# Earlier bias transfers, a staircase moved to VectorE and lent PSUM banks in a fused attention and feed-forward kernel

## The chip, the cores and the metric

The kernel runs on one core of one Trainium2 chip. The metric is the device time of the core in microseconds (us), median of several runs. Ratios are the mean time of one kernel's fast runs over that of the other's of the same rounds, so they are not quite the ratio of the medians that stand beside them. Under 1 is faster. A ratio comes with a 95% interval.

TensorE does the matmuls, VectorE (DVE) and ScalarE (ACT) empty PSUM, GpSimd (POOL) casts inputs and issues small transfers, SyncE (SP) issues the large loads.

## The reference, cut to what matters

```
scores = q k^T / 8                       # 8 x 8 heads, 576 positions, 64 wide, causal
bias   = -(cum[i] - cum[j]),  cum = cumsum(max(s, 0))
attn   = softmax(scores + min(bias, 0))
x      = attn v, heads side by side      # 4608 x 512
h      = x w_in                          # 512 -> 2048
out    = (h * clip(h + 3, 0, 6) / 6) w_out
```

The kernel handles heads in 32 pairs. The feed-forward part, two chains of 512-wide matmuls, is cut into groups that are slipped between the attention steps from pair 4 on. TensorE does all of both.

## The kernel before

The bias enters the scores as four more rows of q and k (rows 64 to 67 of a qk buffer; a constant "staircase" of rows stands behind them, from row 68 on), and a small transfer per head, called aug below, puts them there. There are three qk buffers. The kernel uses eight PSUM banks: two each under the names s, ph and po, one each under t and o. `ph` and `po` belong to the first and the second matmul of the feed-forward part.

```python
def load_aug(p, eng):                       # the bias rows of a pair
    for hh in range(2): eng.dma_start(out=qks[p % NQK][64:68, hh, ...], in_=aug[2*p+hh ...])

def t_bank(other, name):                    # where a transpose lands
    if early[0] and other:                  # early: pairs 0 to 3
        return psum.tile([128, 640], F16, tag="po", bufs=2, name=name)
    return psum.tile([128, 640], F16, tag="t", name=name)

def transpose(p, i):                        # i = 0: q, 1: k;  pairs 0 to 8
    ...                                     # six PE transposes into t_bank(i == 1)
    copy = (nc.vector.tensor_copy, nc.scalar.copy)[i]
    for hh in range(2): copy(out=qk[0:64, hh, i, ...], in_=pt[...])

def av(p, hh, part):                        # attention times v
    if part == 0:
        tag = "t" if hh and p > NPE else "o"
        O[p, hh] = psum.tile([128, 5, 65], F32, tag=tag, bufs=1, name="O")
    ...
for p in range(NP):
    cast_qk(p + 2, gpsimd, gpsimd)          # GpSimd
    if p == 0: set_stair(2, gpsimd)
    else: cast_v(p + 1)
    load_aug(p + 2, nc.gpsimd)
    next_weights(...)                       # GpSimd issues these too
    ...                                     # SyncE: loads of pair p + 3
    if p < PPB:                             # pairs 0 to 3: attention alone
        scores(p,0,0); scores(p,0,1); get(0); scores(p,0,2); corner(p)
        av(p-1,1,0); av(p-1,1,1); norm(p-1,1)
        scores(p,1,0); get(1); scores(p,1,1)
        transpose_x(p-1)
        av(p,0,0); scores(p,1,2); av(p,0,1); norm(p,0)
        continue
    ...                                     # from pair 4 on, with group() between the steps
    corner(p); get(1); group(); scores(p,1,0); group(); ...
```

`get(i)` transposes q or k of the next pair (from pair 9 on it spreads what a DMA transpose brought). `norm` divides by the row sums on VectorE, and `transpose_x` needs its result. `scores(p, hh, 0)` ends with a minimum against a mask on VectorE, `corner` with a smaller one.

The softmax here doesn't subtract the row's maximum and nothing guards it: scores larger than these inputs give would overflow.

Of the kernel before, what the change touches and what calls it, by code (L numbers as in the profile page):

```python
# [9 lines left out]
F32 = mybir.dt.float32  # L10
# [8 lines left out]
def kernel(  # L19
# [10 lines left out]
    nc = tc.nc  # L30
# [7 lines left out]
    NP = NHEADS // 2  # L38
# [92 lines left out]
            in_=v[b, h0 : h0 + 2, 512:SEQ, :].rearrange("h p d -> p h d"),  # L131
        )

    def load_aug(p, eng):
        for hh in range(2):
            g = 2 * p + hh
            eng.dma_start(  # L137
                out=qks[p % NQK][64:68, hh, :, 64 * hh : 64 * hh + SEQ],
                in_=aug[g : g + 1, :, :, :],
            )  # L140
# [39 lines left out]
    def cast_qk(p, eng_q, eng_k):  # L180
        tok = work.tile([128, 24 * D], F16, tag="tok", name="tok")
        if p < NPE:
            tok = tok[0:96].rearrange("p (i e h d) -> p i e h d", i=2, e=6, h=2)
            for i, eng in enumerate((eng_q, eng_k)):
                eng(out=tok[:, i].rearrange("p t h d -> p h t d"), in_=raw6(p)[:, i])  # L185
        else:
            tok = tok[:, 0 : 18 * D]
            for i, eng in enumerate((eng_q, eng_k)):
                eng(  # L189
                    out=tok[:, 9 * D * i : 9 * D * (i + 1)],  # L190
                    in_=raws[p % NRAW][:, 9 * D * i : 9 * D * (i + 1)],
                )
        toks[p] = tok

    def cast_v(p):
        vraw, va = vraws[p % NRAW], vas[p % NQK]
        nc.gpsimd.tensor_copy(out=va[:, :, 0:4, 0:64], in_=vraw[:, :, 0:4, :])  # L197
        nc.gpsimd.tensor_copy(out=va[0:64, :, 4, 0:64], in_=vraw[0:64, :, 4, :])
# [8 lines left out]
        return psum.tile(shape, F32, tag=tag, bufs=2, name=name)  # L207

    def t_bank(other, name):
        if early[0] and other:  # L210
            return psum.tile([128, 640], F16, tag="po", bufs=2, name=name)
        return psum.tile([128, 640], F16, tag="t", name=name)

    def transpose(p, i):
        tok, qk = toks[p], qks[p % NQK]
        pt = t_bank(i == 1, "pt")
        for e in range(6):
            nc.tensor.transpose(  # L218
                pt[:, 96 * e : 96 * (e + 1)],
                tok[:, i, e].rearrange("p h d -> p (h d)"),  # L220
                ident[0:96, 0:96],
            )
        copy = (nc.vector.tensor_copy, nc.scalar.copy)[i]
        for hh in range(2):
            r = 64 * hh
            copy(  # L226
                out=qk[0:64, hh, i, r : r + SEQ].rearrange("p (t e) -> p t e", e=6),
                in_=pt[r : r + 64, 0:SEQ].rearrange("p (e t) -> p t e", e=6),
            )
# [37 lines left out]
    def scores(p, hh, g):  # L267
        qT, kT = qk_of(p, hh)
        pt = Pof(p, hh)
        S = s_bank([128, 512], "S")  # L270
        if g == 0:
            for j in range(4):
                c = slice(128 * j, 128 * (j + 1))
                mm(S[:, c], lhsT=kT[:, c], rhs=qT[:, c], start=(j == 0), stop=(j == 3))  # L274
        else:
            for j in ((0, 3) if g == 1 else (1, 2)):
                c = OFF[j] - 512 * g
                w = 448 - 128 * j
                mm(  # L279
                    S[:, c : c + w],  # L280
                    lhsT=kT[0:68, 128 * j : 128 * (j + 1)],
                    rhs=qT[0:68, 128 * (j + 1) : SEQ],
                    start=(c == 0),
                    stop=(c != 0),
                )
        c = slice(512 * g, 512 * (g + 1))
        nc.scalar.activation(out=pt[:, c], in_=S, func=AF.Exp, scale=0.125)  # L287
        if g == 0:
            nc.vector.tensor_tensor(  # L289
                out=pt[:, c], in0=pt[:, c], in1=masks[:, c], op=ALU.min  # L290
            )
# [22 lines left out]
    def av(p, hh, part):  # L314
        va, pt = vas[p % NQK], Pof(p, hh)
        if part == 0:

            tag = "t" if hh and p > NPE else "o"
            O[p, hh] = psum.tile([128, 5, 65], F32, tag=tag, bufs=1, name="O")
        o = O[p, hh]  # L320

        def block(i, j, lhsT, **kw):
            mm(o[:, i, :], lhsT=lhsT, rhs=va[:, hh, j, 0:65], **kw)  # L323

        def off(i, j):
            c = OFF[j] + 128 * (i - j - 1)
            block(i, j, pt[:, c : c + 128], start=False, stop=False)

        if part == 0:
            for j in range(4):  # L330
                block(j, j, pt[:, 128 * j : 128 * (j + 1)], start=(j == 0), stop=False)
            for i in range(1, 5):
                off(i, 0)
        else:
            for i, j in ((2, 1), (3, 1), (4, 1), (3, 2), (4, 2), (4, 3)):
                off(i, j)
            c = 64 * hh
            block(4, 4, PCs[p % 2][:, c : c + 128], start=False, stop=True)
# [103 lines left out]
    def group():  # L442
        a, c = m1_ready(), m2_ready()
        if not (a or c):
            return False
        if a and (last[0] == 2 or (tail[0] and not c)):
            m1(*m1_list[done[1]])
            done[1] += 1
            last[0] = 1
        else:  # L450
            if c:
                m2(*m2_list[done[2]])
                done[2] += 1
            last[0] = 2
        return True
# [16 lines left out]
    def set_stair(i, copy):  # L472
        for hh in range(2):
            copy(
                out=qks[i][64:128, hh, :, 64 * hh : 64 * hh + 640].rearrange(
                    "p i (t c) -> p i t c", c=128
                ),
                in_=stair_sb[64:128, :, None, :].to_broadcast([64, 2, 5, 128]),
            )
# [36 lines left out]

    cast_qk(0, nc.scalar.copy, nc.scalar.copy)
    transpose(0, 0)
    load_aug(0, nc.scalar)
    transpose(0, 1)  # L520
    cast_v(0)
    cast_qk(1, nc.gpsimd.tensor_copy, nc.gpsimd.tensor_copy)
    next_weights(1)
    load_aug(1, nc.gpsimd)
    cast_v(1)


    for p in range(NP):
        nxt = p + 1 < NP
        if p + 2 < NP:  # L530
            cast_qk(p + 2, nc.gpsimd.tensor_copy, nc.gpsimd.tensor_copy)
            if p + 2 >= NPE:
                crossbar_qk(p + 2)
        if p == 0:
            set_stair(2, nc.gpsimd.tensor_copy)
        elif nxt:
            cast_v(p + 1)
        if p + 2 < NP:
            load_aug(p + 2, nc.gpsimd)
        next_weights(1 if p < 3 else 2 if p < 4 else 3)  # L540
        for m in (p + 3, p + 4):
            if m < NP and (m < NPE) == (m == p + 3):
                for i in range(2):
                    load_qk(m, i, nc.sync)
        if p + 3 < NP:
            load_v(p + 3, nc.sync)

        def get(i):
            if p + 1 < NPE:
                transpose(p + 1, i)  # L550
            elif nxt:
                spread(p + 1, i)

        if p < PPB:
            scores(p, 0, 0)
            scores(p, 0, 1)
            get(0)
            scores(p, 0, 2)
            corner(p)
            if p:  # L560
                av(p - 1, 1, 0)
                av(p - 1, 1, 1)
                norm(p - 1, 1)
            scores(p, 1, 0)
            get(1)
            scores(p, 1, 1)
            if p:
                transpose_x(p - 1)
            av(p, 0, 0)
            scores(p, 1, 2)  # L570
            av(p, 0, 1)
            norm(p, 0)
            continue

        if p == PPB:
            av(p - 1, 1, 0)
            av(p - 1, 1, 1)
            norm(p - 1, 1)
            scores(p, 0, 0)
            scores(p, 0, 1)  # L580
            transpose_x(p - 1)
            early[0] = False
            scores(p, 0, 2)
            get(0)
            group()
            group()
        else:
            scores(p, 0, 0)
            get(0)
            group()  # L590
            scores(p, 0, 1)
            av(p - 1, 1, 0)
            group()
            scores(p, 0, 2)
            av(p - 1, 1, 1)
            norm(p - 1, 1)
            group()
        corner(p)
        get(1)
        group()  # L600
        if p > NPE:
            x_done[0] = p - 1
        scores(p, 1, 0)
        group()
        scores(p, 1, 1)
        av(p, 0, 0)
        if p > PPB:
            (crossbar_x if p >= NPE else transpose_x)(p - 1)
        group()
        scores(p, 1, 2)  # L610
        group()
        av(p, 0, 1)
        norm(p, 0)
        group()
# [40 lines left out]
```

## Time and profile before

| | before |
|---|---|
| time, median of 4 runs | 371.19 us (370.39 to 371.49) |
| span of the profiled run | 367.8 us, TensorE busy 340.9 |
| first scores | 13.59 us |
| first group of the feed-forward part | 38.89 us |
| mean granted TensorE clock | 0.995 |

Two more lines of its page, beside those in the prediction. The first is the chain of work that ended last, as shares of the span by engine. The second is the clock that TensorE was granted, in tenths of full speed per slice of 9.2 us (the digit 8 is one stretch at half speed: 0.75 over the 6.77 us of pair 3 makes about 3.4 us, an estimate).

```profile
PE 80%; DVE 7%; DMA 7%; POOL 2%; ACT 2%; issue 1%; SPq 0%; POOLq 0%; ACTq 0%
PEclk9998999999999999999999999999999999999999
```

### The profile page before, as it was taken

How to read it: one execution, taken by the hardware profiler on the slowest of the kernel's cores; microseconds unless marked ns; L12 is line 12 of the kernel's file. 1: busy time of each engine (PE TensorE's matmuls, PEld its weight loads, DVE VectorE, ACT ScalarE, POOL GpSimd, SP SyncE). 2: the span in 40 equal slices, each digit the busy share in tenths (PEclk: the TensorE clock that was granted, in tenths of full speed). 3: DMA queues.
4: the chain of work that ended last, by engine and by line, in shares of the span. 5: the costliest groups of instructions: out<-in, count | busy, mean ns of one | idle time of the engine just before them, and what ended most of it. 6: DMA issues, size and time to landing. Idle time of an engine off the chain costs nothing.

```text
span 367.8 us, 7622 instructions
## 1 busy us (share of the span) xinstructions
PE 340.9 (93%) x2841; PEld 190.6 (52%) x2841; DVE 242.3 (66%) x544; ACT 225.8 (61%) x392; POOL 120.4 (33%) x217
## 2 busy tenths in 40 slices
PE   1486888999998999999999999999999999999995
PEld 0475555555555555555555555555555444444442
DVE  7477688687778777777777777777775644544531
ACT  6577789766667666666666666666666343343310
POOL 3997694643335342433334333332000000000000
PEclk9998999999999999999999999999999999999999
DMA  8999999999999898998999979987411010010012
GB/s 203 239 229 241 223 229 175 189 192 215 201 176 172 158 192 165 191 177 173 183 153 200 179 165 189 179 176 127 80 48 46 30 57 29 30 59 29 30 57 86
DMA packets 150589, 54.01 MB, mean 147 GB/s; under 512 B 137808, under 2 KB 145632, under 8 KB 150552
## 3 DMA queue, kind: packets, MB, share of 16 engines
q1 hardware_dynamic: 143616, 48.17, 67.5%
q0 software_dynamic: 6272, 4.78, 7.8%
q10 hardware_dynamic: 664, 0.58, 0.6%
q8 instruction: 22, 0.36, 0.4%
q14 instruction: 15, 0.12, 0.1%
HBM read 37.11 MB, written 9.44 MB: 127 GB/s over the span
## 4 chain that ended last, share of the span: by engine, by line
PE 80%; DVE 7%; DMA 7%; POOL 2%; ACT 2%; issue 1%; SPq 0%; POOLq 0%; ACTq 0%
PE po L406 33%; PE ph L386 31%; PE O L323 6%; PE S L279 6%; DMA qk<-aug 3%; DMA vraw<-in_v_dram 3%; PE S L274 3%; DVE gT L395 1%; DVE P L289 1%; DVE qk L226 1%; POOL tok L185 1%; DVE x L346 1%; DVE qk L249 1%; ACT P L287 1%; ACT tr L394 1%
## 5 line engine op out<-in xcount | busy, mean ns | idle before, releaser
L395 DVE SCALAR_TENSOR_TENSOR gT<-tr,ph 128x512 f16<-128x512 f32 x144 | 98.9, 687 | 95.6 <-ACT tr L394 92.2
L386 PE MATMUL ph<-xT,w_in_sb 128*128 128x512 f16 x576 | 147.9, 379 | 0.7 <-DVE gT L395 0.5
L394 ACT ACTIVATE tr<-ph,bias 128x512 f32<-128x512 f32 x144 | 99.0, 688 | 79.7 <-PE ph L386 71.7
L406 PE MATMUL po<-w_out_sb,gT 128*128 128x512 f16 x576 | 145.5, 379 | 0.0
L287 ACT ACTIVATE P<-S 128x512 f16<-128x512 f32 x192 | 112.0, 595 | 39.9 <-PE S L274 22.8
L406 PEld LDWEIGHTS <-gT 128*128 128x128 f16 x576 | 50.3, 97 | 46.1
L386 PEld LDWEIGHTS <-w_in_sb 128*128 128x128 f16 x576 | 51.1, 97 | 44.3 <-issue 0.7
L137 POOL DMA_DIRECT2D qk<-aug x62 | 36.3, 587 | 65.4 <-PE S L279 50.9
L279 PE MATMUL S<-qk 68*128 68x448 f16 (+3 forms) x256 | 51.2, 282 | 0.4 <-ACT P L287 0.2
L323 PE MATMUL O<-va,P 128*128 128x65 f16 x896 | 49.0, 195 | 2.4 <-DVE x L346 2.4
L323 PEld LDWEIGHTS <-P 128*128 128x128 f16 x896 | 40.5, 99 | 16.1 <-DVE x L346 3.6
L197 POOL CAST va<-vraw 128x512 f16<-128x512 f32 x32 | 20.1, 629 | 56.0 <-PE O L323 50.3
L279 PEld LDWEIGHTS <-qk 68*128 68x128 f16 x256 | 24.5, 102 | 24.4 <-issue 1.2
L289 DVE TENSOR_TENSOR P<-P,masks_sb 128x512 f16<-128x512 f16 x64 | 30.4, 476 | 7.3 <-ACT P L287 7.2
L189 POOL CAST tok<-raw 128x576 f16<-128x576 f32 x46 | 29.9, 672 | 12.5 <-DMA raw<-in_q_dram 4.3
L346 DVE TENSOR_TENSOR x<-O,rl 128x320 f16<-128x320 f32 x64 | 31.4, 491 | 2.2
L249 DVE COPY qk<-jt 64x768 f16<-64x768 f16 x92 | 30.7, 334 | 1.7
L274 PE MATMUL S<-qk 128*128 128x128 f16 x256 | 26.0, 227 | 5.9 <-DMA qk<-aug 5.1
L415 DVE TENSOR_SCALAR ob<-po 128x512 f32<-128x512 f32 x36 | 24.6, 682 | 9.5 <-PE po L406 9.5
L274 PEld LDWEIGHTS <-qk 128*128 128x128 f16 x256 | 19.8, 101 | 18.7 <-issue 6.4
L218 PE MATMUL pt<-ident,tok 96*128 96x96 f16 x108 | 9.5, 237 | 10.7 <-ACT tok L185 7.8
L185 POOL CAST tok<-raw 96x768 f16<-96x768 f32 x16 | 13.2, 842 | 6.2 <-PE ptx L360 3.0
(39 smaller groups left out, 141.4 us busy)
## 6 DMA issues: line engine op xcount, KB each, us to landing
raw<-in_q_dram SPq DMA_DIRECT2D x32, 288.0 KB, 3.9
out_dram<-ob SPq DMA_DIRECT2D x36, 256.0 KB, 2.3
raw<-in_k_dram SPq DMA_DIRECT2D x31, 288.0 KB, 7.4
vraw<-in_v_dram SPq DMA_DIRECT2D x64, 128.0 KB, 4.5
w_in_sb<-in_moe_w_in_dram POOLq DMA_DIRECT2D x4, 512.0 KB, 9.8
w_out_sb<-in_moe_w_out_dram POOLq DMA_DIRECT2D x8, 256.0 KB, 8.7
vraw<-in_v_dram SPq DMA_DIRECT2D x32, 32.0 KB, 3.7
qk<-aug POOLq DMA_DIRECT2D x62, 9.0 KB, 3.5
```

The lines of the kernel that those rows point to most:

```text
L137: eng.dma_start(out=qks[p % NQK][64:68, hh, :, 64 * hh : 64 * hh + SEQ], in_=aug[g : g + 1, :, :, :],)
L249: nc.vector.tensor_copy(out=qk[0:64, :, i, 128 * par : 128 * par + 256 * n].rearrange("p h (s two c) -> p h s two c", two=2, c=128)[:, :, ...
L274: mm(S[:, c], lhsT=kT[:, c], rhs=qT[:, c], start=(j == 0), stop=(j == 3))
L279: mm(S[:, c : c + w], lhsT=kT[0:68, 128 * j : 128 * (j + 1)], rhs=qT[0:68, 128 * (j + 1) : SEQ], start=(c == 0), stop=(c != 0),)
L287: nc.scalar.activation(out=pt[:, c], in_=S, func=AF.Exp, scale=0.125)
L289: nc.vector.tensor_tensor(out=pt[:, c], in0=pt[:, c], in1=masks[:, c], op=ALU.min)
L323: mm(o[:, i, :], lhsT=lhsT, rhs=va[:, hh, j, 0:65], **kw)
L346: nc.vector.tensor_tensor(out=X[p][:, :, hh, :], in0=o[:, :, 0:64], in1=rl.to_broadcast([128, 5, 64]), op=ALU.mult,)
L386: mm(ph, lhsT=w_in_sb[:, kc, ft * 128 : (ft + 1) * 128], rhs=xT[:, kc, n * 512 : (n + 1) * 512], start=(kc == 0), stop=(kc == NKC - 1),)
L394: nc.scalar.activation(out=tr, in_=ph, func=AF.Relu, bias=bias3[:, 0:1])
L395: nc.vector.scalar_tensor_tensor(out=gTs[n][:, ft, :], in0=tr, scalar=6.0, in1=ph, op0=ALU.min, op1=ALU.mult)
L406: mm(po, lhsT=gTs[n][:, ft, t4 * 128 : (t4 + 1) * 128], rhs=w_out_sb[:, ft, :], start=(ft == 0), stop=(ft == NFT - 1),)
```

## The change

The intent: bias transfers are issued ahead of the casts in GpSimd's program, pair 0's on two queues. VectorE, idle at that time, makes the third staircase. The idle banks of the second matmul hold the k and x transposes (before, only those of pairs 0 to 3) and the second head's output until the second matmul starts. Half of the k copies of odd pairs goes from ScalarE to VectorE. Cut to its core:

```diff
-        if early[0] and other:
+        if not done[2] and other:
             return psum.tile([128, 640], F16, tag="po", bufs=2, name=name)
...
-        copy = (nc.vector.tensor_copy, nc.scalar.copy)[i]
         for hh in range(2):
+            on_act = i == 1 and (hh == 0 or p % 2 == 0)
+            copy = nc.scalar.copy if on_act else nc.vector.tensor_copy
...
-            tag = "t" if hh and p > NPE else "o"
-            O[p, hh] = psum.tile([128, 5, 65], F32, tag=tag, bufs=1, name="O")
+            tag = "o" if not hh or 0 < done[2] and p <= NPE else "t" if p > NPE else "po"
+            O[p, hh] = psum.tile(
+                [128, 5, 65], F32, tag=tag, bufs=2 if tag == "po" else 1, name="O"
+            )
...
-    load_aug(0, nc.scalar)
+    load_aug(0, (nc.scalar, nc.gpsimd))
     transpose(0, 1)
+    set_stair(2, nc.vector.tensor_copy)
     cast_v(0)
+    load_aug(1, (nc.gpsimd, nc.gpsimd))
     cast_qk(1, nc.gpsimd.tensor_copy, nc.gpsimd.tensor_copy)
...
         if p + 2 < NP:
+            load_aug(p + 2, (nc.gpsimd, nc.gpsimd))
             cast_qk(p + 2, nc.gpsimd.tensor_copy, nc.gpsimd.tensor_copy)
-        if p == 0:
-            set_stair(2, nc.gpsimd.tensor_copy)
-        elif nxt:
+        if p and nxt:
             cast_v(p + 1)
-        if p + 2 < NP:
-            load_aug(p + 2, nc.gpsimd)
...
         corner(p)
-        get(1)
         group()
         scores(p, 1, 0)
+        get(1)
         group()
```

Below, "bias part" means the bias issues and the staircase, "bank part" the banks and the later place of `get(1)`.

More of the change, by code (lines that the diff above doesn't have):

```diff
@@ L132, in load_v, with load_aug @@
         )
-    def load_aug(p, eng):
-        for hh in range(2):
+    def load_aug(p, engs):
+        for hh, eng in enumerate(engs):
             g = 2 * p + hh
@@ L518 @@
     transpose(0, 0)
-    load_aug(0, nc.scalar)
+    load_aug(0, (nc.scalar, nc.gpsimd))
     transpose(0, 1)
+    set_stair(2, nc.vector.tensor_copy)
     cast_v(0)
+    load_aug(1, (nc.gpsimd, nc.gpsimd))
     cast_qk(1, nc.gpsimd.tensor_copy, nc.gpsimd.tensor_copy)
     next_weights(1)
-    load_aug(1, nc.gpsimd)
     cast_v(1)
```

## The prediction

> **What bounds the kernel now.** I read the page first. Its two lines of totals:
>
> ```profile
> PE 340.9 (93%) x2841; PEld 190.6 (52%) x2841; DVE 242.3 (66%) x544; ACT 225.8 (61%) x392; POOL 120.4 (33%) x217
> PE   1486888999998999999999999999999999999995
> ```
>
> TensorE is busy for 340.9 of 367.8 us, and the second line (tenths of busy time in 40 slices) puts its holes into the first third. From there on the end moves only with TensorE's work, which this change leaves as it is (the same 5684 rows in its program, some in another order). So at most the 26.9 us of TensorE's idle time is on offer. The stretches view says where it lies: 12.2 us are before 13.6 us, when the first scores start (7.83 before the first transpose, 4.36 before the scores, little more); some 4 us after the last matmul; 10.7 us between 13.6 and 122 us; from 120 to 280 us there is none. The end needs no look: its last output transfer is not touched.
>
> I then cut the span at the first score matmul of each pair of heads. Columns: stretch, its length, then busy time of TensorE (instructions), its weight loads, VectorE, ScalarE, GpSimd, then granted clock, DMA share, GB/s:
>
> ```profile
> 13.59:18.83 5.24, 4.65 (x46) 3.77 (x46) 3.95 (x5) 4.33 (x9) 5.17 (x8) 1.00 1.19 237
> 18.83:25.19 6.36, 5.58 (x66) 4.62 (x66) 5.13 (x13) 4.93 (x10) 6.32 (x11) 1.00 1.24 225
> 25.19:30.38 5.19, 3.44 (x66) 2.89 (x66) 3.61 (x9) 4.22 (x9) 4.33 (x8) 1.00 1.18 245
> 30.38:37.15 6.77, 5.50 (x80) 4.72 (x81) 5.03 (x12) 5.02 (x10) 5.04 (x8) 0.75 1.20 234
> 37.15:45.04 7.89, 6.59 (x73) 3.99 (x69) 5.16 (x11) 6.33 (x12) 5.78 (x9) 1.00 1.24 231
> 45.04:52.80 7.76, 6.91 (x82) 4.44 (x81) 6.43 (x15) 6.99 (x14) 6.85 (x11) 1.00 1.20 222
> 52.80:60.56 7.76, 6.91 (x82) 4.45 (x81) 6.60 (x15) 6.99 (x14) 3.29 (x6) 1.00 0.97 175
> 60.56:70.27 9.71, 8.62 (x90) 5.22 (x89) 7.64 (x17) 7.32 (x14) 5.20 (x10) 1.00 1.14 206
> ```
>
> Pairs 0 to 3 have attention alone, pairs 4 to 7 have first-matmul groups beside it. TensorE's idle time here (length less busy) is 0.59, 0.78, 1.75, 1.27, 1.30, 0.85, 0.85 and 1.09 us. What ended it, from the timeline, in the brackets:
>
> ```profile
> 13.59 0.59 PE L274 MATMUL S<-qk 128*128 128x128 f16 x4 [4.36 <-DMA qk<-aug]
> 18.73 0.23 PE L323 MATMUL O<-va,PC 128*128 128x65 f16 x1 [0.59 <-DVE PC L308]
> 25.19 0.38 PE L274 MATMUL S<-qk 128*128 128x128 f16 x4 [0.78 <-DMA qk<-aug]
> 29.11 0.45 PE L360 MATMUL ptx<-ident,x 128*128 128x128 f16 x5 [1.61 <-DVE x L346]
> 36.67 0.60 PE L323 MATMUL O<-va,P 128*128 128x65 f16 x14 [0.82 <-DVE x L346]
> 40.76 0.42 PE L218 MATMUL pt<-ident,tok 96*128 96x96 f16 x6 [0.78 <-POOL tok L185]
> 48.52 0.42 PE L218 MATMUL pt<-ident,tok 96*128 96x96 f16 x6 [0.58 <-POOL va L198]
> 56.29 0.41 PE L218 MATMUL pt<-ident,tok 96*128 96x96 f16 x6 [0.58 <-DVE qk L226]
> 64.30 0.42 PE L218 MATMUL pt<-ident,tok 96*128 96x96 f16 x6 [0.83 <-DVE qk L226]
> ```
>
> The last four are one wait: the k transpose wants the single t bank, which VectorE is still emptying of q (its copies end at 40.61, 48.47, 56.23, 64.24). The two rows that name GpSimd are misread releasers; its casts for that pair ended by 32.1 us for the first of them.
>
> **What the Trainium skill says.** (1) "DMA: Bandwidth & Descriptors", section "Issuing engines are not separate DMA queues": starting transfers from several engines saves only issue time. The trace agrees so far: the two bias transfers of pair 0 on ScalarE's queue were issued at 8.31 and about 9.6 us and took about 5.2 us each, as the large loads beside them did (4.7 to 4.9), since the engines are full (share above 1.1). (2) "SBUF — State Buffer", "SBUF: two separate sides": VectorE operations with two SBUF inputs and GpSimd lock each other out. The trace agrees: the mask minimum at 14.84 us took 1.45 us beside a GpSimd cast and 0.41 at 18.60; the corner's minimum at 17.76 took 0.91 beside GpSimd's staircase copy and 0.21 elsewhere. (3) "TensorE: Matmul & The Clock Gate", Part 1: half clock until a window of about 3.4 us was busy. The trace: the 128x64 and 128x448 pair of matmuls took 0.63 us until 22.9 us and 0.38 after, and the 30.38 stretch shows clock 0.75.
>
> **The change, part by part.**
>
> *Bias of pair 0 on two queues.* The first score waits only for head 0, still issued by ScalarE at 8.31 after the bias rows are ready at 8.14. It lands near 13.5 as before. Head 1 leaves GpSimd at about 8.2 instead of ScalarE at 9.6, with some 6 us to landing (GpSimd's took 5.7 to 7.4): 14.3, before its first use at 15.2. The first weight load (512 KB) leaves 1.2 us later, behind two more bias issues of 0.58 us, so a little less traffic is about: 0.1 us.
>
> *Third staircase on VectorE.* 2.53 us leave GpSimd at 16.07 and become about 1.0 us of VectorE at 10.1 (as its first, 2 x 0.5), where VectorE sits idle until 14.84. It frees GpSimd and the lock, so the corner's minimum takes 0.2 instead of 0.9. The 0.59 at 18.73 largely goes. But the odd pair's k half, 0.75 us, comes into VectorE's queue just there: 0.3 us.
>
> *Bias ahead of casts.* Pair 2's bias was issued at 18.54 behind casts and staircase and landed at 25.15; now it goes at about 14.5 and lands by 21. The 0.78 goes, but ScalarE's exponentials of pair 1 last until 25.0, so the chain gains not 0.8 but 0.6. Pair 3's (22.86 to 30.24, on the chain of waits) had landed 0.1 us before TensorE came to it, so no more is gained than not being held later. The 1.61 at 29.11 stays: scores, exponential, mask, 1.51 of q copies, corner, reciprocal, product are a chain through VectorE of 3.9 us.
>
> *Banks lent.* The second head's output no longer waits for the first head's normalisation. At 36.67 half of the 0.82 is covered by the exponentials, which end at 36.5 anyway: 0.5 us. For pairs 4 to 7 the k transposes get a second-matmul bank and come one group later. Their waits sum to 0.78 + 0.58 + 0.58 + 0.83 = 2.77, and three waits of 0.26 to 0.27 for the output bank go too: 3.56.
>
> *k copies shared.* An odd pair moves 0.64 us from ScalarE to 0.75 us on VectorE. ScalarE's 6.99 of 7.76 becomes 6.35 in the 52.80 stretch, but VectorE's 6.60 becomes 7.35. So that pair can fall to about 7.4, not to TensorE's 6.91; the 45.04 one (even, ScalarE 6.99) to about 7.2; 37.15 to 7.1 and 60.56 to 8.95. That is 0.4 + 0.55 + 0.8 + 0.75 = 2.5 us of the 3.56.
>
> *Later groups.* The k spread now follows the next mask and the group's product, so of the 0.53 us wait for the product at 119.35 I take 0.4. Later stretches have no idle time.
>
> Sum: 0.1 + 0.3 + 0.6 + 0.5 + 2.5 + 0.4 = 4.4 us. I take off 0.3 for the k half in VectorE's chain of pairs 1 and 3, and for GpSimd, which now waits for the previous pair's last score before it may cast. 371.2 - 4.1 = 367.1 us.
>
> **Rivals.** (a) *DMA is the early bound.* It moves 220 to 245 GB/s through the first 50 us. Then earlier compute would wait for loads, and about 369.5 would be left. For it: loads issued at 22.7 take 11.8 us. Against it: pair 6's q lands near 38.5 and is transposed at 45.3, so about 5 us of slack exist. (b) *The blocked GpSimd queue turns on us*: casts behind a bias that waits for scores come later, and so do raw buffers and loads: 369 to 372. Against it: the casts of pairs 3 and 5 wait for their loads anyway. (c) *The clock*: with the gaps at 18.73 and 25.19 gone, the half-speed window of 30.4 to 33.8 vanishes or warm-up comes a window sooner; each window holds up to 1.5 us of extra matmul time, most of it now hidden in the VectorE chain. With all of TensorE's waits gone as well: 364.5. The reverse, one more cold window, costs about as much.
>
> **Range and chances.** The floor is about all early waits except the 29.11 one gone (some 6.7 us, 364.5); the ceiling is gains only at the bank (369.6). Faster by over 2% needs under 363.8, which needs every term in full and a clock window: 7%. Slower by 2% has no mechanism of that size: 2%.
>
> **What would show it.** First score still near 13.5; no wait on the bias at pair 2's first score; no wait on q copies at the k transposes of pairs 5 to 8; first product of the second matmul near 62 instead of 65.64; VectorE the busiest helper where an odd pair is copied. It is wrong if the first score moves by over 1 us, if TensorE's waits before 70 us stay above 7 us in sum after 13.6 (8.5 now), or if new idle time turns up after 120 us.

## The result, and the profile after

The changed kernel takes 369.81 us (368.89 to 370.07, 4 runs) against 371.19 us. The ratio is 0.9962, interval 0.9938 to 0.9986. That is 1.4 us where 4.1 were predicted, and just outside the range. In a later call it was 0.9984 (0.993 to 1.0038).

First, the lines of its page that answer to those above: engine totals, TensorE's busy tenths, its clock, and the chain by engine.

```profile
PE 341.5 (93%) x2841; PEld 191.7 (52%) x2841; DVE 250.1 (68%) x550; ACT 222.8 (61%) x388; POOL 117.0 (32%) x216
PE   1478988899998999999999999999999999999995
...
PEclk9995899999999999999999999999999999999999
...
PE 83%; DVE 9%; ACT 4%; DMA 2%; issue 1%; ACTq 0%
```

Transfers fall from 7% to 2% of the chain, as intended. But VectorE's and ScalarE's shares rise together by about as much as TensorE's, and the clock row holds a 5 and an 8 where there was one 8: from the clocks below some 10.2 us at half speed instead of 3.4 (an estimate). The record misses the start, where the clock reads 1.00 while matmuls take the half-speed time. By the matmuls' own durations TensorE was slow for about 17 us (14.35 to 21.4 and 28.8 to 38.5) instead of about 13 (13.6 to 23.5 and 30.4 to 33.9). TensorE is busy for longer (341.5) although its work is the same.

The stretches from pair to pair, same columns as in the prediction:

```profile
14.35:18.76 4.41, 4.41 (x45) 3.72 (x46) 3.12 (x6) 3.50 (x8) 4.41 (x8) 1.00 1.16 223
18.76:24.19 5.43, 4.61 (x69) 3.93 (x67) 4.66 (x11) 4.48 (x9) 4.86 (x8) 1.00 1.18 237
24.19:30.55 6.36, 4.08 (x72) 3.54 (x69) 5.50 (x11) 3.85 (x10) 4.32 (x7) 0.83 1.20 230
30.55:37.95 7.40, 6.91 (x84) 5.88 (x82) 6.19 (x12) 5.29 (x10) 4.63 (x8) 0.50 1.24 235
37.95:44.63 6.68, 6.63 (x71) 4.17 (x69) 5.96 (x13) 5.45 (x11) 5.34 (x9) 0.95 1.23 231
44.63:52.62 7.99, 6.79 (x82) 4.45 (x81) 7.18 (x15) 7.21 (x14) 6.43 (x11) 1.00 1.21 211
52.62:59.85 7.23, 6.80 (x82) 4.45 (x81) 7.05 (x16) 6.34 (x13) 4.66 (x9) 1.00 1.16 202
59.85:69.74 9.89, 8.53 (x91) 5.21 (x90) 7.80 (x17) 7.17 (x14) 4.28 (x8) 1.00 0.99 200
```

Pairs 0 and 1 are 0.83 and 0.93 us shorter than before (5.24 and 6.36). Pairs 2 and 3 are 1.17 and 0.63 us longer (5.19 and 6.77), and pair 3 runs wholly at clock 0.50. Pairs 4 to 7 take 31.79 us together instead of 33.12. TensorE's waits, from its timeline:

```profile
14.35 0.58 PE L275 MATMUL S<-qk 128*128 128x128 f16 x4 [5.11 <-DMA qk<-aug]
23.21 0.45 PE L363 MATMUL ptx<-ident,x 128*128 128x128 f16 x5 [0.82 <-DVE x L349]
28.77 0.72 PE L363 MATMUL ptx<-ident,x 128*128 128x128 f16 x5 [2.28 <-DVE x L349]
35.25 0.72 PE L363 MATMUL ptx<-ident,x 128*128 128x128 f16 x5 [0.49 <-DVE x L349]
50.17 0.45 PE L363 MATMUL ptx<-ident,x 128*128 128x128 f16 x5 [1.20 <-DVE x L349]
57.40 0.45 PE L363 MATMUL ptx<-ident,x 128*128 128x128 f16 x5 [0.43 <-DVE x L349]
65.09 1.04 PE L409 MATMUL po<-w_out_sb,gT 128*128 128x512 f16 x4 [1.36 <-DVE x L349]
...
118.73 0.34 PE L275 MATMUL S<-qk 128*128 128x128 f16 x3 [0.92 <-DVE qk L250]
```

Every wait that the change aimed at is gone: the bias at pair 2, the corner minimum, the four on the t bank, the output bank. In their place stand waits for one thing, x on VectorE: the normalisation, met at the x transpose, and at 65.09 by the first second-matmul, whose bank still holds the last lent output. From 76 to 109 us the changed kernel is 0.86 us ahead (pair 12's second-head scores start at 108.76 instead of 109.61). At 118.73 it waits for the k spread, and by 123.7 us the lead is 0.03. So the changed kernel's run stands against the other as follows: start 0.76 us lost, pairs 0 to 3 0.04 lost, pairs 4 to 7 1.33 won, pair 8 0.33 won, pairs 9 to 14 0.83 lost. They end at the same span, 367.8 us; the medians differ by 1.4.

### The profile page after: what moved, and what is told of

Its sections match the earlier page's. It is cut to its first block, busy times and chain, and to the rows that moved or that the text cites. A ratio compares the mean times of both kernels' runs of the same rounds, so it can differ in the third digit from the quotient of the medians.

```text
span 367.8 us, 7616 instructions
## 1 busy us (share of the span) xinstructions
PE 341.5 (93%) x2841; PEld 191.7 (52%) x2841; DVE 250.1 (68%) x550; ACT 222.8 (61%) x388; POOL 117.0 (32%) x216
## 4 chain that ended last, share of the span: by engine, by line
PE 83%; DVE 9%; ACT 4%; DMA 2%; issue 1%; ACTq 0%
PE po L409 33%; PE ph L389 30%; PE O L326 7%; PE S L280 7%; PE S L275 3%; DVE qk L227 2%; DVE gT L398 2%; DMA qk<-aug 2%; DVE P L290 2%; ACT P L288 1%; DVE x L349 1%; PE ptx L363 1%; DVE qk L250 1%; ACT qk L477 1%; ACT tr L397 1%
## 5 line engine op out<-in xcount | busy, mean ns | idle before, releaser
L326 PE MATMUL O<-va,P 128*128 128x65 f16 x896 | 50.2, 198 | 0.0
L326 PEld LDWEIGHTS <-P 128*128 128x128 f16 x896 | 41.8, 101 | 13.3 <-DVE x L349 0.2
L250 DVE COPY qk<-jt 64x768 f16<-64x768 f16 x92 | 31.6, 344 | 1.3
L227 DVE COPY qk<-pt 64x576 f16<-64x576 f16 x22 | 16.5, 752 | 0.5 <-PE pt L218 0.3
```

The lines of the kernel that those rows point to most:

```text
L250: nc.vector.tensor_copy(out=qk[0:64, :, i, 128 * par : 128 * par + 256 * n].rearrange("p h (s two c) -> p h s two c", two=2, c=128)[:, :, ...
L326: mm(o[:, i, :], lhsT=lhsT, rhs=va[:, hh, j, 0:65], **kw)
```

## The experiments

All variants gave correct results. Each call had its own runs of the kernel before on the same chip (its median is given); times of one kernel in one call spread over 1 to 5 us, so ratios within about 0.3% of each other are not told apart unless the intervals say so. My first theories were four: the first bias lands later because the loads go ahead of it (the start); the early gain goes into VectorE's chain, the lock between VectorE and GpSimd and half-speed windows; the bank gain goes into new waits on VectorE; the lead is lost at the batch boundary near 118 us (pairs 13 and 14; in pair 13 no feed-forward group is ready for some 3 us).

### Call 1: parts of the change (before: 370.88 us)

**a_bias**: the kernel before with the bias part alone.

```diff
 before.py + only the load_aug and set_stair lines of the change
```

> The kernel before with the bias and staircase parts alone (bias issues first, pair 0 on two queues, third staircase on VectorE); PSUM banks, k transpose place and k copies as before. Theory A (the start and the early stage cost what the early issue gains): the first score starts near 14.3 us instead of 13.6, pair 2 starts without a wait for the bias, and the time is within 0.3% of before. Rival B (these parts are the whole gain, and the bank part gives nothing or costs): ratio near 0.996, like the full change.

Measured: 372.59 us, ratio 1.0039 (0.9996 to 1.0081). The first score started at 12.82 us, pair 2 at 23.19 instead of 25.19 and without a wait for the bias. Half of that lead was gone at pair 3 (29.40 against 30.38); the rest held to pair 5 (44.00 against 45.04) and turned into a loss of 3.2 us by pair 7 (63.80 against 60.56). The start did not move as theory A had it, and B's gain did not come: the part predicted at 1.0 us of gain is no gain alone. Its trace shows one way of losing (timeline; VectorE's mask minimum, GpSimd's q and k casts, and the k transpose on TensorE):

```profile
54.38 2.14 DVE L289 TENSOR_TENSOR P<-P,masks_sb 128x512 f16<-128x512 f16 x1
54.59 1.60 POOL L185 CAST tok<-raw 96x768 f16<-96x768 f32 x2
...
58.00 0.64 PE L218 MATMUL pt<-ident,tok 96*128 96x96 f16 x6 [2.30 <-DVE qk L226]
```

A minimum of 0.41 us takes 2.14 beside two casts. The q copies behind it, and the transpose that waits for them, move by as much.

**b_bias0_act**

```diff
-    load_aug(0, (nc.scalar, nc.gpsimd))
+    load_aug(0, (nc.scalar, nc.scalar))
```

> The changed kernel, with both bias transfers of pair 0 back on ScalarE's queue. Theory A (taking a transfer out of the hardware queues let the loads of pair 2 go ahead of the first bias, which then lands later): k of pair 2 is issued near 9.6 us again, the first score comes near 13.6 instead of 14.35, and up to 0.7 us of time is won, ratio 0.995 to 0.996 against before. Rival B (the later landing is the luck of one execution, or comes from GpSimd's two bias transfers of pair 1): first score still near 14.3, time as the full change.

Measured: 367.86 us, ratio 0.9941 (0.9903 to 0.998), first score at 13.61. By itself that fits A, but a_bias and d_spread_back, with two queues, started at 12.82 and 13.15. See the note on the start after call 4.

**c_banks**: the kernel before with the bank part alone.

```diff
 before.py + only the t_bank, av and get(1) lines of the change (k copies all on ScalarE)
```

> The kernel before with the bank part alone (idle second-matmul banks lent to the k transpose, the x transpose and the second head's output; k copy one group later), k copies all on ScalarE, bias as before. Theory A (the four waits on the t bank go, but at pairs 4 to 7 a wait on VectorE's normalisation takes their place, 1.2 us at one x transpose and 1.4 us at the first second-matmul): 1 to 1.5 us won by pair 8, at most 0.5 us of it left after the batch boundary near 118 us, ratio 0.997 to 1.000. Rival B (the replacement waits come from the shared k copies, which are absent here): 2.5 us won, ratio near 0.993.

Measured: 368.46 us, ratio 0.9932 (0.9907 to 0.9956). This is 2.5 us, B's number, although the waits on the normalisation that A named are there (1.19 at an x transpose, 0.92 at the first second-matmul): the replacement waits do not come from the shared copies. A was wrong about the boundary: with bias as before, no wait stands there, and pair 14's scores follow at their shortest distance (4.64 us from one head to the other, 5.33 before). So the bank part alone is worth as much as the whole change, or more.

**d_spread_back**

```diff
         corner(p)
+        if p + 1 >= NPE: get(1)
         group()
         scores(p, 1, 0)
-        get(1)
+        if p + 1 < NPE: get(1)
```

> The changed kernel, with the k spread of the pairs from 9 on (the second call of get) back ahead of the group and the scores, where it was before. Theory A (the 0.86 us lead that the changed kernel has until 108 us is lost near 118 us because the moved spread runs into GpSimd's casts, 2.49 us instead of 0.7): the wait of 0.92 us for the spread is gone, 0.5 to 0.9 us won on the full change, ratio near 0.994. Rival B (at the batch boundary something else, GpSimd's casts or the loads, holds both kernels to the same time, so any lead is lost there): the wait moves to another row, time as the full change, 0.996.

Measured: 369.60 us, ratio 0.9948 (0.9909 to 0.9988). The wait for the spread is 0.44 instead of 0.92, with 0.58 for the product behind it: 0.15 us gained at the boundary, and nothing clear in the time. The place of the spread is at most a small part of the cause. Three kernels at the boundary, the k spread on VectorE in each: the changed kernel, with a GpSimd cast beside it,

```profile
116.17 2.49 DVE L250 COPY qk<-jt 64x768 f16<-64x768 f16 x2
116.69 1.28 POOL L189 CAST tok<-raw 128x576 f16<-128x576 f32 x2
```

the kernel before,

```profile
116.88 1.49 DVE L249 COPY qk<-jt 64x768 f16<-64x768 f16 x2
```

and c_banks, where the cast comes only at 119.42:

```profile
117.62 0.67 DVE L249 COPY qk<-jt 64x768 f16<-64x768 f16 x2
```

The same two copies take 0.67 or 2.49 us depending on where GpSimd's casts fall.

### Call 2: the early stage (before: 370.63 us)

**after_again**: the changed kernel, unedited.

> The changed kernel once more, unedited, as the control of this call. The first score started at 14.35 us in its first profile but at 12.8 and 13.15 in two variants with the same program up to there. If the start is luck, it lies anywhere from 12.8 to 14.4 here; if the change delays it, near 14.35 again. Ratio near 0.996.

Measured: 369.99 us, ratio 0.9984 (0.993 to 1.0038), first score 14.31, mean clock of six runs 0.986 where the kernel before had 0.993. At half speed (the 0.50 above) 0.007 of 369 us is an estimated 5 us more in the cold state, which costs at most half of that; the record's blind start makes this rough. Its profile fell on a bad run, and shows the early chain at its worst:

```profile
20.09 2.03 DVE L290 TENSOR_TENSOR P<-P,masks_sb 128x512 f16<-128x512 f16 x1
20.23 1.60 POOL L185 CAST tok<-raw 96x768 f16<-96x768 f32 x2
...
24.49 0.45 PE L363 MATMUL ptx<-ident,x 128*128 128x128 f16 x5 [3.07 <-DVE x L349]
...
26.29 1.60 POOL L185 CAST tok<-raw 96x768 f16<-96x768 f32 x2
26.63 2.33 DVE L290 TENSOR_TENSOR P<-P,masks_sb 128x512 f16<-128x512 f16 x1 [0.24 <-ACT P L288]
...
31.33 0.71 PE L363 MATMUL ptx<-ident,x 128*128 128x128 f16 x5 [3.56 <-DVE x L349]
```

Casts and mask minimum of pairs 1 and 2 start within 0.35 us of each other, the minimum loses 1.6 and 1.9 us, and TensorE stands for 3.07 and 3.56 us at the x transpose; after the second its matmuls are slow (0.71 us at 31.33 for five transposes that took 0.45 at 24.49). In the profile of before, the minima of those pairs took 0.42 and 0.49 us:

```profile
20.08 0.42 DVE L289 TENSOR_TENSOR P<-P,masks_sb 128x512 f16<-128x512 f16 x1 [0.32 <-ACT P L287]
...
26.24 0.49 DVE L289 TENSOR_TENSOR P<-P,masks_sb 128x512 f16<-128x512 f16 x1 [1.07 <-ACT P L287]
```

The traces show that this is more than one bad run. In pair 1 the minimum took 0.42 us in all four kernels with the bias behind the casts (before, c, m, n), and 0.98 on average (0.41 to 2.03) in the sixteen profiles with the bias ahead of them there. In pair 2 it is 0.56 (eight profiles, i, j, k and q among them) against 1.10 (twelve).

**i_order**

```diff
-            load_aug(p + 2, ...)            # ahead of cast_qk, every p
+            if p < 2: load_aug(p + 2, ...)  # ahead of cast_qk
...
+        if 2 <= p < NP - 2: load_aug(p + 2, ...)   # behind cast_v
```

> The changed kernel with the bias issue put back behind the casts from pair 4 on (pairs 0 to 3 stay early). Theory A (the bias ahead of the casts makes GpSimd wait for the last score of the previous pair, so that its casts start with the pair and lock VectorE out of its mask minimum: 1.45 and 2.14 us instead of 0.41 in the bias-alone variant): the minimum's excess between 37 and 70 us falls from 1.2 to 3.3 us to under 0.8, and 0.2 to 0.4% is won on the control of this call. Rival B (which instruction collides is luck; the bias order is neutral): within 0.1% of the control.

Measured: 368.97 us, ratio 0.9941 (0.9894 to 0.9987), the wait at the boundary gone (4.64 us between the heads). But the minima between 37 and 70 us took 5.91 us where eight of 0.41 would take 3.3, an excess of 2.6 (one of 2.29 at 45.10), against A. The interval of the control overlaps this one. Inconclusive.

**g_warm_first**: fillers, whose results nobody reads.

```diff
     transpose(0, 1)
+    for _ in range(44): nc.tensor.transpose(spare[:, 0:128], ident, ident)
...
             if p:
+                for _ in range(10): mm(<bank of O[p, 0]>, lhsT=ident, rhs=masks[:, 0:325])
                 transpose_x(p - 1)
```

> The changed kernel with filler on TensorE that computes nothing used: 44 transposes while it waits for the first bias and 10 matmuls of 325 columns ahead of each of the first three x transposes, where it waits for VectorE. Theory A (part of the gain went into half-speed windows, granted clock 0.984 over the span against 0.995 before): the clock is 0.998 or more, matmuls of pairs 0 to 3 take 0.22 to 0.38 us per group instead of 0.6, and 1 to 2 us are won on the control. Rival B (in the early stage VectorE's chain is the bound, and a faster TensorE only waits longer for it): clock up, but under 0.5 us won.

Measured: 367.57 us, ratio 0.9903 (0.9864 to 0.9943), clock 0.999, and six runs within 1.1 us where the control's spread over 5.3. More instructions, and 2.4 us faster than the control: A's case, and a little more than its number. The intervals of the two overlap at their edges, so that half-speed windows are part of the loss is likely, not shown.

**h_late_ptx**

```diff
             scores(p, 1, 1)
-            if p: transpose_x(p - 1)
             av(p, 0, 0); scores(p, 1, 2); av(p, 0, 1); norm(p, 0)
+            if p: transpose_x(p - 1)
             continue
```

> The changed kernel with the x transpose of the early pairs moved behind the pair's last attention-value matmuls, so that TensorE does not stand still for VectorE's normalisation (waits of 0.82, 2.28 and 0.49 us in the changed kernel). Theory A (the VectorE chain of q copies, corner minimum and normalisation, met in order by TensorE, is what bounds pairs 1 to 3): 1.5 to 3 us won on the control, ratio near 0.990. Rival B (loads or ScalarE bind next): the waits turn up in front of the scores or the k transpose, under 0.5 us won.

Measured: 367.36 us, ratio 0.9895 (0.9854 to 0.9937), 2.6 us faster than the control. A's number again. One line moved, at work in pairs 1 to 3 only, wins more than the whole change did.

### Call 3: shared copies, fillers, combinations (before: 370.82 us)

**e_k_act**

```diff
-            on_act = i == 1 and (hh == 0 or p % 2 == 0)
+            on_act = i == 1
```

> The changed kernel with all k copies back on ScalarE. Theory A (the shared copy, 0.75 us more on VectorE for every odd pair, lengthens the chain that TensorE waits for): 0.2 to 0.4% better than the changed kernel (0.9962 and 0.9984 in its two calls), ratio near 0.994, x-transpose waits of pairs 1 and 3 shorter. Rival B (ScalarE relieved is worth as much as VectorE burdened): ratio 0.996 to 0.999 as the full change.

Measured: 370.32 us over all six runs, two slow; ratio of the other four 0.9948 (0.9901 to 0.9995). The x-transpose wait of pair 2's turn was 0.16 but that of pair 1's 2.45. Inconclusive: the shared copy is worth too little to be seen here.

**f_warm**: the changed kernel with the ten-matmul fillers of g_warm_first alone, not the 44.

```diff
 after.py + only the second filler of g_warm_first
```

> The changed kernel with the filler ahead of the first three x transposes alone (10 matmuls each), none at the start. Theory A (what the full filler won, 2.4 us of medians, is the half-speed windows after the x-transpose waits): 1 us or more better than the changed kernel, ratio near 0.993, clock over 0.995. Rival B (the win was the warm start of pairs 0 and 1): ratio 0.996 to 0.999, clock as the changed kernel's.

Measured: 369.14 us, ratio 0.9957 (0.993 to 0.9984), clock 0.999. That is between A and B: a warm clock in pairs 1 to 3 without a warm start is no clear gain, since the x-transpose waits remain:

```profile
29.46 0.45 PE L373 MATMUL ptx<-ident,x 128*128 128x128 f16 x5 [1.46 <-DVE x L348]
35.58 0.45 PE L373 MATMUL ptx<-ident,x 128*128 128x128 f16 x5 [1.46 <-DVE x L348]
```

At full clock pairs 2 and 3 took 6.12 and 7.06 us, only 0.24 and 0.34 less than in the changed kernel; before, 5.19 and 6.77. The mask minimum took 1.61 us in both pairs of this run. So a full clock does not help much where VectorE's chain is long. What the warm start of g adds stays open: k_combo_warm and p_late_warm have it too and do not gain.

**j_combo**

```diff
 after.py + h_late_ptx + i_order, and
-            tag = "o" if not hh or 0 < done[2] and p <= NPE else ...
+            tag = "o" if not hh or 6 <= p <= NPE else ...
```

> The changed kernel with three repairs: the x transpose of early pairs late, the bias behind the casts from pair 4 on, and the second head's output of pairs 6 and 7 back in its own bank so that the first second-matmul does not wait for a normalisation (1.1 to 1.4 us in all variants with the lent bank). If the repairs add: late x transpose 0.6 to 0.9%, boundary 0.2%, first second-matmul 0.2 to 0.3%: ratio 0.985 to 0.988, no wait of over 0.5 us at the first second-matmul, none for the k spread near 116 us. If one bound takes over from another: 0.989 or more, and the waits move to another row of pairs 4 to 7.

Measured: 368.91 us, ratio 0.9942 (0.9916 to 0.9968). The wait at the first second-matmul is gone, but pair 9's scores start at 75.59, later than in h_late_ptx (73.76), though pair 7's started within 1.3 us of it. The repairs do not add.

**k_combo_warm**: j_combo and the 44 filler transposes.

```diff
 j_combo + the first filler of g_warm_first
```

> The three repairs and the 44 filler transposes before the first score. If the cold start still costs beside the repairs: 0.2 to 0.4% better than them alone, clock 0.997 or more. If VectorE and ScalarE bound pairs 0 and 1 once TensorE is at full clock: within 0.1% of the repairs alone.

Measured: 369.19 us, ratio 0.9947 (0.9914 to 0.998), clock 0.989, so neither expectation's clock. It is the earliest of all at pair 8 (65.79 us, before 70.27) but has lost most of that at pair 9 (76.61, before 77.31). VectorE there waits for the k spread's source:

```profile
68.99 1.02 DVE L250 COPY qk<-jt 64x768 f16<-64x768 f16 x2 [1.25 <-DMA jt<-tok]
```

Pair 9 is the first that comes by DMA transpose. Here its casts waited for their loads until 61.35 us, and SyncE issued the transpose at 65.50. That is rival (a) of the prediction, loads as the bound, at a place where I had not looked. It is no fixed limit: in h_again (call 4) SyncE issued the transpose at 62.57, nothing waited for it, and pair 9 started at 72.83.

### Call 4: is the bias part worthless, or swallowed? (before: 370.20 us)

**m_before_late**, **o_bias_late**, **n_banks_late**, **h_again** (5 runs): the late x transpose on the kernel before, on the bias part, on the bank part, and on the full change.

```diff
 before.py / a_bias / c_banks / after.py + the lines of h_late_ptx
```

> The kernel before with the late x transpose of the early pairs alone. Theory A (before, the waits were spread over bias, corner minimum, bank and x transpose; the change gathered them in front of the x transpose): 0.2 to 0.4% won, as the x transpose had only 1.61 + 0.45 us of wait there and the next wait is near. Rival B (the x transpose is the common bound of both kernels): 0.7 to 0.9% won, as on the changed kernel.

> The bias and staircase part with the late x transpose. Theory A (its gain was swallowed by that wait): at least 0.4% better than the kernel before with the late transpose. Rival B (the bias ahead of the casts does harm in itself, through GpSimd's casts and the port lock): no better than the kernel before with the late transpose, ratio 0.995 or more.

> The bank part with the late x transpose, bias as before. If the bias part is worth something once the wait is gone, this is 0.2% or more behind the full change with the late transpose; if it is worthless or harmful, this is equal to it or better (0.989 or less).

> The full change with the late x transpose once more, the control of this call: 0.9895 in its first call, so 0.986 to 0.993.

| | x transpose as it was | x transpose late (call 4) |
|---|---|---|
| before | 1 | 1.0010 (0.9989 to 1.0031), 370.97 us |
| bias part | 1.0039 (0.9996 to 1.0081) | 0.9992 (0.9963 to 1.0021), 370.37 us |
| bank part | 0.9932 (0.9907 to 0.9956) | 0.9947 (0.9922 to 0.9973), 368.25 us |
| full change | 0.9962 and 0.9984 | 0.9905 (0.9888 to 0.9922), 367.20 us; 0.9895 in call 2 |

The late transpose is worth nothing on the kernel before, so B of m falls; A's 0.2 to 0.4% did not come either. On the bank part it is worth nothing. It pays only in the full change. Read along the last column, what the full change has over the bank part is worth 0.4% (0.9947 to 0.9905, the intervals just touch), the first case of n's expectation. That is the bias part and the shared k copies together: n has no shared copies. Its trace speaks for the bias part, as TensorE there waits 2.20, 0.84 and 0.40 us for the bias at pairs 1 to 3. On the kernel before the bias part is worth 0.2%, unclear, and A of o (0.4%) was missed. The traces say why. With the bias part but one output bank, o_bias_late only moves the wait, from the transpose to the output bank that the same normalisation must free (L323 is attention times v):

```profile
22.63 0.62 PE L323 MATMUL O<-va,P 128*128 128x65 f16 x8 [2.00 <-DVE x L346]
28.88 0.42 PE L323 MATMUL O<-va,P 128*128 128x65 f16 x8 [1.45 <-DVE x L346]
34.20 0.42 PE L323 MATMUL O<-va,P 128*128 128x65 f16 x8 [2.04 <-DVE x L346]
```

With lent banks and the late place, h_again, the wait for the output bank is gone and 0.55 us is left at the transpose:

```profile
22.33 0.45 PE L363 MATMUL ptx<-ident,x 128*128 128x128 f16 x5 [0.55 <-DVE x L349]
26.69 0.45 PE L363 MATMUL ptx<-ident,x 128*128 128x128 f16 x5 [0.55 <-DVE x L349]
31.89 0.45 PE L363 MATMUL ptx<-ident,x 128*128 128x128 f16 x5 [0.55 <-DVE x L349]
```

Its pairs start at 12.81, 17.23, 22.84, 28.04 and 33.23 us, the last against 37.15 before and 37.95 in the changed kernel; the profiled run was at full clock throughout (1.000).

**The start.** In twelve profiles with pair 0's bias on two queues and no filler at the start the first score began between 12.81 and 15.06 us, mean 13.9; in five with both on ScalarE between 12.26 and 13.88, mean 13.2. The ranges overlap. So the 14.35 of the first profile is mostly luck of the transfers; whether two queues cost half a microsecond is left open. They gain nothing that can be seen.

### Call 5: on top of the best (before: 370.46 us)

**p_late_warm** and **q_late_order**

```diff
 h_late_ptx + the 44 filler transposes / h_late_ptx + the lines of i_order
```

> The full change with the late x transpose and the 44 filler transposes before the first score. If the half-clock start is worth something beside the late transpose: 0.2 to 0.4% better than 0.9895 and 0.9905, so 0.986 to 0.988, clock 0.998 or more. If ScalarE and VectorE, or the loads near 65 us, bind instead: 0.989 to 0.991.

> The full change with the late x transpose and the bias issue behind the casts from pair 4 on. Theory A (the order costs 0.9 to 1.2 us at the batch boundary): no wait of over 0.5 us for the k spread near 116 us and 0.2 to 0.3% won, 0.987 to 0.988. Rival B (the later bias brings a wait of its own at pairs 5 to 9, as 1.89 and 0.78 us in the combinations): the boundary wait gone, but 0.989 to 0.993.

Measured: 368.75 us, 0.9939 (0.9894 to 0.9984), clock 0.989; and 368.25 us, 0.9936 (0.9888 to 0.9984). Neither improves on the late transpose, nor is either told apart from it on another chip. In q the boundary wait is gone, but pair 9 starts at 77.22 us: a lead won behind the boundary was lost before it, B's case. The order's cost alone stays unsettled.

The best kernel is the changed one with the late x transpose: 0.9905 and 0.9895, intervals clear of the changed kernel's first ratio only at their edge (0.9922 against 0.9938), and of the kernel before by far.

## Why the prediction was wrong, point by point

**Right:** TensorE's idle time before 122 us was the only thing on offer; the bias wait at pair 2, the corner wait and the four t-bank waits all went. None of the three signs of being wrong came (the first score moved by 0.76 us, the waits before 70 us sum to 6.6, no idle time is new after 120), but the first second-matmul came at 65.09, not near 62.

**Right by luck:** by pair 2 the changed kernel was 1.0 us ahead, the 0.1 + 0.3 + 0.6 predicted. It had started 0.76 late and won 1.76 in pairs 0 and 1, and only 0.55 of that was idle time (1.37 to 0.82), as a new wait of 0.82 at the x transpose stood where the bias wait had been. The other 1.21 was busy time: the matmuls left half speed at about 21.4 us instead of 23.5.

**The step that failed** is the sentence "The 1.61 at 29.11 stays: scores, exponential, mask, 1.51 of q copies, corner, reciprocal, product are a chain through VectorE of 3.9 us." I had found the chain and taken it as fixed, and then added gains in front of it. It took 4.58 us in the changed kernel's first profile (24.19 to 28.77) and 5.86 in the second (25.47 to 31.33). In the traces what lengthens it is mostly GpSimd's casts beside VectorE's minima: the mask minimum took 0.77, then 2.33 us where it had taken 0.49, and in the first profile the corner's 0.47 instead of 0.21. The exponential ahead of them came only 0.1 us later.

```profile
25.00 0.83 POOL L185 CAST tok<-raw 96x768 f16<-96x768 f32 x1
25.36 0.77 DVE L290 TENSOR_TENSOR P<-P,masks_sb 128x512 f16<-128x512 f16 x1 [0.25 <-ACT P L288]
```

TensorE then stood in one piece for 2.3 to 3.6 us, where before it had stood in three, and ran at half speed afterwards for longer than before: rival (c) in the reverse form that it named. In the first profile pair 2 so gave back all that pairs 0 and 1 had won, and 0.2 us more: 0.66 by the longer chain and 0.51 by slower matmuls behind it. The table of call 4 shows that a gain was there and was swallowed: with the x transpose out of the way the same change gives 0.9905, about 3.5 us, against 4.1 predicted. How this divides between the wait and the half speed that follows it is not shown.

**Mis-sized:** the bank term for pairs 4 to 7. Of 3.56 us of waits I booked 2.5; in the trace of the changed kernel 1.33 came (33.12 to 31.79). Pairs 4 and 6 fell further than booked (6.68 and 7.23 us), pairs 5 and 7 grew (7.99 and 9.89). The step was to subtract waits and cap the rest by busy time. The three that came in their place (1.20, 0.43, 1.36) sum to 2.99, all for VectorE's normalisation, which stands in VectorE's order behind the copies; a busy share of 7.2 of 8.0 us does not show order. The first second-matmul could have been foreseen: a lent bank must come back before its owner's first use, and j_combo, which returns it earlier, has no wait there. The bank part by itself was worth 0.7%.

**Wrong in sign:** the 0.4 us at 119 us. The wait of 0.53 for the product became 0.92 for the spread and 0.25 for the product, because GpSimd's casts now fell on the spread. In the six kernels with the late `get(1)` but bias behind the casts (c, i, j, k, n, q) no wait of this kind stands there; in those with bias first it does.

**Mis-sized without cost:** the staircase on VectorE took 3.81 us, not 1.0, beside GpSimd's cast and issues; VectorE had nothing else to do until 15.60.

**Rival (b)**, the blocked GpSimd queue, was nearer the truth than I gave it credit for, but by another path: not late casts but casts at a worse moment. That the minima lengthen with the bias ahead of the casts, the twenty traces show (0.42 against 0.98 us in pair 1). What it costs in time they do not: i_order and q_late_order, made to isolate it, did not come clear of the noise, so that share of the cause stays open. So does the worth of the shared k copies.

## What to carry to other kernels

When several waits of an engine are removed, look for what they were hiding: here the same engine met VectorE's normalisation a few instructions later, and in the early pairs the gain went there until that meeting point was moved. A change of order on an engine off the critical path (GpSimd's bias before its casts) also decides at which moment its long instructions hold a shared port, so check what they will now coincide with. Where runs differ by as much as the effect, profile the control again, and judge a part of a change in the company of the other parts as well as alone.

## What the Trainium skill lacked or had wrong

- "SBUF — State Buffer", "SBUF: two separate sides", says that the loser of the shared port blocks for the whole instruction. Here a VectorE minimum of 0.41 us took 2.03 us beside two successive GpSimd casts (1.60 us in all) and 2.33 us beside four (26.29 to 28.67), so it sat through more than one, and two staircase copies took 3.81 instead of 0.93 us beside casts and transfer issues. The page does not say that a waiting instruction can lose to the next one too.
- "TensorE: Matmul & The Clock Gate", Part 1, gives a busy window of about 3.4 us as enough for full clock. With TensorE busy without a gap from the first score, the matmuls here left the half-speed time after 3.6 us (e_k_act), 5.0 (after_again), 7.1 (the changed kernel) and 7.7 us (h_late_ptx). The page has its windows run freely, so that up to two of them, 6.8 us (an estimate from its figure), may pass; the last two lie above even that. With filler from 9.03 us on (g_warm_first) they took 0.38 us from the first scores at 13.53. The clock record of those stretches reads 1.00 while the matmuls were slow; that fits the page's warning that such records have been unreliable.
- No page says how much the landing of a small transfer varies behind loads: the same first bias on two queues let the scores start between 12.8 and 15.1 us from profile to profile.
